# Three banks in turn for the third layer of the first expert, the conversions among them

## The chip, the core and the metric

The kernel runs on one core of a Trainium2 chip. Four of the core's engines compute: TensorE (PE in the profile; its weight loads are PEld), VectorE (DVE), ScalarE (ACT) and GpSimd (POOL). SyncE (SP) and POOL also issue transfers. PE writes its products to PSUM, a small memory of eight banks, from which DVE and ACT read. The metric is the device time of one launch in microseconds.

## What is computed

Three stages, each fed by the one before. Stage two sends each of 3072 tokens to one of eight experts of 384 tokens each, and every expert passes two matrices; stage three passes the tokens through two more, with a rational function between. The kernel does stages two and three expert by expert.

```python
# 1: attention with a decaying state, y of shape (4, 8, 768, 64)
state = gamma * state + outer(k[t], v[t]);  y[t] = scale * q[t] @ state
# 2: experts, x of shape (3072, 512); a greedy choice by x @ w_gate, 384 tokens each
h = np.maximum(x[mask] @ w1[e], 0.0)        # 512 -> 1024
out[mask] = h @ w2[e]                       # 1024 -> 512
# 3: rational network
h = x @ w_in                                # 512 -> 2048
P = a[0] + a[1] * h + a[2] * h2 + a[3] * h3
Q = 1.0 + np.abs(b[0]) * np.abs(h) + np.abs(b[1]) * h2
g = P / (Q + 1e-06)
out = g @ w_out                             # 2048 -> 512
```

## The kernel before

**Stages.** The first 168 us are the attention; the routing follows, and then eight experts, n = 0 to 7. Each matrix product is made of three passes over numbers split in a high and a low part (`split`, `three`). An expert has two halves. In the first, `mm1` (w1) and `mm2` (w2) alternate over 8 blocks of 128 columns. In the second, `mm3` (w_in) and `mm4` (w_out) run over 16 blocks i: `mm3(n, i)` writes one PSUM bank of 128x384; `rat1` to `rat3` and `gsplit` make the rational function of it; `mm4(n, i - 3)` uses the result three blocks later. PE's round is therefore mm3 of block i, mm4 of block i - 3.

**A block's way.** mm3 is 12 matmuls at L840. ACT reads the bank three times (L894 to L896). POOL adds (L897). DVE reads the bank twice (L898, L899); the bank is free when L899 has ended. Meanwhile ACT makes a reciprocal by logarithm and exponential (L908, L909), DVE refines and applies it (L914 to L916), ACT and POOL split the result (L921, L922), and mm4 (L936) takes it.

**Banks.** Of the eight banks four are sums (`acc0` to `acc3`), one is for the routing (`pr`), two have the name `w` and one the name `x`. `wtile` hands out `w` and `x`: it counts in `WN[0]`, and each third tile is `x`, so that three banks take turns. With `first=True`, which `mm1` and `mm3` of the first expert pass, it doesn't count and always gives one of the two `w`.

**Conversions.** Weights arrive as 64-bit numbers. Most blocks of w_in are converted in the attention stage; the six blocks in `NORES` (5, 7, ... 15) are converted in the first expert's second half, between its blocks: `in_conv_a(j)` calls `conv`, which works on DVE in three steps (L243, L245 and L246, in the profile CUSTOM_DVE_ANT_0) with one step on ACT (L244). Its middle value is in the bank that `ctile` gives, which is `x`; L243 and L245 write it, L246 reads it last. `in_conv_b` splits the result (L249 on ACT, L250 on POOL) into the tile `wis`, which the block's mm3 reads, and `in_store` sends it to memory for the later experts. Conversion j is asked for behind block 1 + 2j.

**The next expert.** While an expert runs, the routing for the next is chosen in small steps (`Chain`): PE's L641, L654, L690 and L691, L721, L731 and, on DVE, the rows between L576 and L745; its products lie in `pr`. `xt` transposes the next expert's tokens (L824 to L827) behind blocks 12 to 14; for expert 1 it asks for `x`.

**Order.** PE, ACT and POOL run in the order of the program as written. The order on DVE and SP is made by a scheduler, which knows what each instruction waits for; the routing's steps have a raised priority. A bank that is handed out again is waited for by its next writer until its last reader has ended.

Of the kernel before, what the change touches and what calls it, by code (L numbers as in the profile page):

```python
# [9 lines left out]
F32 = mybir.dt.float32  # L10
# [19 lines left out]
CAP = NT // E  # L30
# [5 lines left out]
KD = DM // 128  # L36
# [140 lines left out]
def moe_kernel(ctx, tc, q, k, v, w_gate, w1, w2, w_in, w_out, a, b, cf, ci, out):  # L177
# [363 lines left out]
    ps = ctx.enter_context(tc.tile_pool(name="ps", bufs=1, space=bass.MemoryType.PSUM))  # L541
# [229 lines left out]
    EV, W1R, W2R, W1S, W2S, XG, XTS, HS, YS, ACC, US, GS, WIS = ({} for _ in range(13))  # L771
# [34 lines left out]
    WN = [0]  # L806

    def wtile(shape, first=False):


        if not first:
            WN[0] += 1
        x = not first and WN[0] % 3 == 0
        return ps.tile(shape, F32, name="x" if x else "w", bufs=1 if x else 2)
# [4 lines left out]
    def xt(n, t):  # L819
        if t == 0:  # L820
            XTS[n] = mp.tile([128, 2, KD, CAP], F32R, name="xT", bufs=1)
        p = ps.tile([128, KD, 128], F32, name="x", bufs=1) if n == 1 else wtile([128, KD, 128])
        for d in range(KD):
            nc.tensor.transpose(p[:, d, :], XG[n][t][:, d * 128:(d + 1) * 128], ident)  # L824
        hi = XTS[n][:, 0, :, t * 128:(t + 1) * 128]
        nc.scalar.activation(hi, p, AF.Copy)  # L826
        nc.vector.tensor_tensor(XTS[n][:, 1, :, t * 128:(t + 1) * 128], p, hi.bitcast(F32), op=OP.subtract)  # L827

    def three(prods, first, last, split=True):

        jobs = [(k, a, b) for k in range(len(prods)) for a, b in ((0, 0), (1, 0), (0, 1))]
        if split:
            jobs.sort(key=lambda t: t[2])
        n = {}
        for k, a, b in jobs:
            o, w, x = prods[k]
            key = id(o)
            n[key] = n.get(key, 0) + 1
            total = 3 * sum(1 for p in prods if p[0] is o)
            nc.tensor.matmul(o, w[a], x[b], start=first and n[key] == 1, stop=last and n[key] == total)  # L840
# [3 lines left out]
    def mm1(n, f):  # L844
        p = wtile([128, CAP], n == 0)
        w, x = W1S[n, f], XTS[n]
        three([(p, (w[:, 0, d * 128:d * 128 + 128], w[:, 1, d * 128:d * 128 + 128]), (x[:, 0, d], x[:, 1, d]))
               for d in range(KD)], True, True)
        h = HS[n, f] = mp.tile([128, 2, CAP], F32R, name="hg", bufs=HGB)
        nc.scalar.activation(h[:, 0], p, AF.Relu)  # L850
        HLO[n, f] = nc.vector.scalar_tensor_tensor(h[:, 1], p, 0.0, h[:, 0].bitcast(F32), op0=OP.max,  # L851
                                                   op1=OP.subtract).ins
        w1_split(n, f + 2)

    def mm2(n, f):
        if f == 0:
            for t in (3, 0, 1, 2):
                ACC[t] = ps.tile([128, 512], F32, name=f"acc{t}")
        w, h = W2S[n, f], HS[n, f]
        three([(ACC[(d + 3) % 4][:, :CAP], (w[:, 0, d * 128:d * 128 + 128], w[:, 1, d * 128:d * 128 + 128]),  # L860
                (h[:, 0], h[:, 1])) for d in range(KD)], f == 0, f == NF1 - 1, f < NF1 - 1)
        w2_split(n, f + 2)
        if f == NF1 - 1:
            y = YS[n] = mp.tile([128, 2, KD, CAP], F32R, name="yT", bufs=1)
            for d in range(KD):
                p = ACC[(d + 3) % 4][:, :CAP]
                nc.scalar.activation(y[:, 0, d], p, AF.Copy)
                nc.vector.tensor_tensor(y[:, 1, d], p, y[:, 0, d].bitcast(F32), op=OP.subtract)

    def wi_load(n, j):  # L870
        if j >= len(NORES):
            return
        i = NORES[j]
        t = WIS[n, i] = mp.tile([128, 2, KD, 128], F32R, name="wis", bufs=NWIS)
        nc.gpsimd.dma_start(t.rearrange("p s a f -> p (s a f)"), wid[i])

    def mm3(n, i):
        p = US[n, i] = wtile([128, CAP], n == 0)
        y = YS[n]
        w = wih[:, RES[i]] if i in RES else WIS[n, i]  # L880
        three([(p, (w[:, 0, d], w[:, 1, d]), (y[:, 0, d], y[:, 1, d])) for d in range(KD)], True, True)
        if n and i not in RES:
            wi_load(n, NORES.index(i) + NWIS)
# [88 lines left out]
    def job_conv(j):  # L972
        if j < NLATE:
            CA[j] = mp.tile([128, KD * 128], I32, name="xg", bufs=TB)
            conv(rawx[:, j % 3], CA[j], mp.tile([128, KD * 128], I32, name="xg", bufs=TB), ctile())
            job_load(j + 3)

    def job_split(j):
        if 0 <= j < NLATE:
            split(woh[:, LATE_OUT[j]], CA[j].bitcast(F32), nc.gpsimd)  # L980
# [3 lines left out]
    def in_load(j):  # L984
        if j >= len(NORES):
            return
        i = NORES[j]
        t = RX[j] = mp.tile([128, KD * 128, 2], I32, name="w2s")
        nc.sync.dma_start(t.bitcast(I64).rearrange("p (a f) o -> p a (f o)", a=KD),
                          w_in[:, i * 128:(i + 1) * 128].rearrange("(a p) f -> p a f", p=128))  # L990

    def in_conv_a(j):
        if j >= len(NORES):
            return
        CA[j] = mp.tile([128, KD * 128], I32, name="w2r")
        conv(RX[j], CA[j], mp.tile([128, KD * 128], I32, name="w2r"), ctile())
        in_load(j + 2)

    def in_conv_b(j):
        i = NORES[j]  # L1000
        w = WIS[0, i] = mp.tile([128, 2, KD, 128], F32R, name="wis", bufs=NWIS)
        w = w.rearrange("p s a f -> p s (a f)")
        split(w, CA[j].bitcast(F32), nc.gpsimd)

    def in_store(j):
        i = NORES[j]
        nc.gpsimd.dma_start(wid[i], WIS[0, i].rearrange("p s a f -> p (s a f)"))
# [27 lines left out]
    def slot(part):  # L1035
        nonlocal credit
        credit += RATE[min(len(ROUTE), 2) - 1][part]
        if credit >= 1:
            credit -= 1
            chain.hop()  # L1040

    for n in range(E):
        last = n + 1 == E
        for f in range(NF1):
            mm2(n, f)
            slot(0)
            if n == 0:
                job_split(f - 1)
                with tc.issue_after(HLO[0, min(f + 1, NF1 - 1)]):
                    job_conv(f)  # L1050
            if f + 2 < NF1:
                mm1(n, f + 2)
                slot(0)
        if n == 0:
            for j in range(2):
                in_load(j)
            for i in range(INA):
                if i in NORES:
                    in_conv_a(NORES.index(i))
            for i in range(INB):  # L1060
                if i in NORES:
                    in_conv_b(NORES.index(i))
            for i in range(INS):
                if i in NORES:
                    in_store(NORES.index(i))
        else:
            for j in range(NWIS):
                wi_load(n, j)
        for i in range(NF2):
            if i > 1:  # L1070
                gsplit(n, i - 2)
            if i:
                rat2(n, i - 1)
                rat3(n, i - 1)
            mm3(n, i)
            slot(1)
            rat1(n, i)
            if i >= LAG:
                mm4(n, i - LAG)
                slot(1)  # L1080
            if n == 0 and i + INA in NORES:
                in_conv_a(NORES.index(i + INA))
            if n == 0 and i + INB in NORES:
                in_conv_b(NORES.index(i + INB))
            if n == 0 and i + INS in NORES:
                in_store(NORES.index(i + INS))
            if n == 0 and i == NF2 - 2:
                for f in range(2):
                    w2_load(1, f)
            if not last:  # L1090
                if i == DUE:
                    begin(n + 1)
                if i - DUE in (0, 1, 2):
                    fetch(n + 1, i - DUE)
                if i - DUE in (2, 3):
                    w1_split(n + 1, i - DUE - 2)
                if i - DUE in (2, 3, 4):
                    xt(n + 1, i - DUE - 2)
        gsplit(n, NF2 - 2)
        rat2(n, NF2 - 1)  # L1100
        rat3(n, NF2 - 1)
        gsplit(n, NF2 - 1)
        for i in range(NF2 - LAG, NF2):
            f = i - NF2 + LAG
            if not last and f < 2:
                mm1(n + 1, f)
                w2_split(n + 1, f)
                slot(1)
            mm4(n, i)
            slot(1)  # L1110
# [26 lines left out]
```

## Time and profile before

| | us |
|---|---|
| time, median of 3 runs | 1068.32 (1067.13 to 1068.67) |
| the profiled execution's own time | 1068.97 |
| its span, from first to last instruction | 1066.0 |
| PE busy | 1008.1 (95%) |
| DVE busy | 758.7 (71%) |
| ACT busy | 697.3 (65%) |
| POOL busy | 622.7 (58%) |

Busy is the time in which an engine works on an instruction; PE counts as busy also where its clock is low. Busy shares are means over stages, so a stage is read from its own stretch of the timeline. The mean granted clock of PE is 0.979 of full speed. The first expert's second half runs from 238.8 to about 318 us.

### The profile page before, as it was taken

To read this page: it belongs to the slowest core of one execution; us is meant where nothing else is said; L and a number is where in the kernel's file an instruction comes from. 1 tells how busy PE (TensorE), PEld (TensorE's weight loads), DVE (VectorE), ACT (ScalarE), POOL (GpSimd) and SP (SyncE) were. 2 spreads that over 40 slices of the span, in tenths; PEclk is the share of its full clock that TensorE was granted. 3 is DMA by queue.
4 is the path that set the end of the run, shared out by engine and by line. 5 is a ranking of instruction groups with operands and counts; after the bars stand their busy time and mean duration, and the time that the engine had idled before them with its cause. 6 is when DMAs were issued, how large, how long until landed. Compare 5 with 4: busy or idle time off the path is not lost.

```text
span 1066.0 us, 18253 instructions
## 1 busy us (share of the span) xinstructions
PE 1008.1 (95%) x6278; PEld 922.1 (87%) x6278; DVE 758.7 (71%) x1841; ACT 697.3 (65%) x1365; POOL 622.7 (58%) x612
## 2 busy tenths in 40 slices
PE   6999994798999999999999999999999999999995
PEld 5888884687789988999899989998999899889984
DVE  4788797579975887588657875887678656751773
ACT  6989991357773687367736873687367737873883
POOL 5667661555685466546654665466546654675452
PEclk9999996799999999999999999999999999999998
DMA  9999963433333221322132223222412241323110
GB/s 193 226 261 259 247 154 108 150 99 102 106 118 110 80 89 58 112 80 89 60 110 79 89 61 113 75 90 59 139 50 91 60 136 53 97 68 118 34 60 30
DMA packets 142027, 115.00 MB, mean 108 GB/s; under 512 B 56560, under 2 KB 122352, under 8 KB 141936
## 3 DMA queue, kind: packets, MB, share of 16 engines
q1 hardware_dynamic: 131184, 76.10, 27.3%
q0 software_dynamic: 10752, 37.75, 10.8%
q8 instruction: 49, 0.80, 0.3%
q14 instruction: 42, 0.34, 0.1%
HBM read 98.10 MB, written 15.73 MB: 107 GB/s over the span
## 4 chain that ended last, share of the span: by engine, by line
PE 72%; DVE 10%; ACT 4%; issue 2%; DMA 1%; POOL 1%; POOLq 0%; DVEq 0%; ACTq 0%
PE w L840 24%; PE acc L936 24%; PE x L840 10%; PE acc L840 8%; PE pr L641 1%; DVE cm L605 1%; DVE hg L851 1%; ACT hg L850 1%; PE pa L384 1%; PE pt L354 1%; PE pr L619 0%; PE w L824 0%; PE x L824 0%; DVE t L898 0%; DVE t L916 0%
## 5 line engine op out<-in xcount | busy, mean ns | idle before, releaser
L936 PE MATMUL acc<-woh,hg 128*128 128x512 f32 x1152 | 289.3, 396 | 0.8 <-ACT hg L921 0.8
L936 PEld LDWEIGHTS acc<-woh,hg 128*128 128x128 f32 x1152 | 213.4, 188 | 43.5 <-ACT hg L921 1.8
L897 POOL TENSOR_TENSOR qq<-qq,z 128x384 f32<-128x384 f32 x127 | 129.0, 1016 | 166.8 <-ACT z L895 165.8
L922 POOL TENSOR_TENSOR hg<-t,hg 128x384 fp32r<-128x384 f32 x127 | 129.5, 1020 | 77.4 <-ACT hg L921 49.0
L840 PE MATMUL acc<-hg,w2s 128*128 128x384 f32 x768 | 145.9, 339 | 0.3 <-DVE hg L851 0.3
L840 PEld LDWEIGHTS acc<-hg,w2s 128*128 128x128 f32 x768 | 132.4, 188 | 1.1 <-DVE hg L851 0.6
L840 PE MATMUL w<-yT,wih 128*128 128x384 f32 x624 | 117.9, 339 | 0.9 <-DVE t L899 0.8
L840 PE MATMUL w<-xT,w1s 128*128 128x384 f32 x600 | 116.6, 343 | 0.6 <-ACT xT L826 0.6
L914 DVE SCALAR_TENSOR_TENSOR qq<-qq,acc 128x384 f32<-128x384 f32 x128 | 70.8, 553 | 59.3 <-ACT acc L909 29.9
L840 PEld LDWEIGHTS w<-yT,wih 128*128 128x128 f32 x624 | 108.1, 188 | 3.6 <-DVE t L899 1.8
L250 POOL TENSOR_TENSOR w1s<-w1r,w1s 128x512 fp32r<-128x512 f32 x64 | 82.6, 1291 | 46.8 <-ACT w1s L249 46.0
L250 POOL TENSOR_TENSOR w2s<-w2r,w2s 128x512 fp32r<-128x512 f32 x64 | 82.6, 1292 | 44.6 <-ACT w2s L249 41.3
L840 PEld LDWEIGHTS w<-xT,w1s 128*128 128x128 f32 x600 | 105.9, 192 | 1.9 <-ACT xT L826 0.8
L921 ACT ACTIVATE hg<-t 128x384 fp32r<-128x384 f32 x128 | 67.2, 525 | 57.7 <-DVE t L916 57.6
L249 ACT ACTIVATE w2s<-w2r 128x512 fp32r<-128x512 f32 x64 | 40.2, 629 | 67.2 <-issue 37.7
L908 ACT ACTIVATE z<-qq,qcb 128x384 f32<-128x384 f32 x128 | 77.7, 607 | 7.9 <-POOL qq L897 7.3
L840 PE MATMUL w<-yT,wis 128*128 128x384 f32 x408 | 78.1, 339 | 3.2 <-DVE t L899 3.2
L916 DVE SCALAR_TENSOR_TENSOR t<-t,ab,acc 128x384 f32<-128x384 f32 x128 | 78.4, 613 | 3.4
L840 PEld LDWEIGHTS w<-yT,wis 128*128 128x128 f32 x408 | 70.9, 188 | 5.8 <-DVE t L899 4.2
L915 DVE SCALAR_TENSOR_TENSOR acc<-qq,acc 128x384 f32<-128x384 f32 x128 | 71.6, 560 | 3.3
L850 ACT ACTIVATE hg<-w 128x384 fp32r<-128x384 f32 x50 | 24.5, 489 | 65.7 <-PE w L840 64.1
L909 ACT ACTIVATE acc<-z 128x384 f32<-128x384 f32 x128 | 63.5, 496 | 4.1
(200 smaller groups left out, 1967.2 us busy)
## 6 DMA issues: line engine op xcount, KB each, us to landing
wis<-wid POOLq DMA_DIRECT2D x42, 512.0 KB, 3.6
w1r<-in_moe_w_dram SPq DMA_DIRECT2D x64, 256.0 KB, 2.8
w2r<-in_moe_w_dram SPq DMA_DIRECT2D x64, 256.0 KB, 2.7
qn<-in_q_dram SPq DMA_DIRECT2D x48, 128.0 KB, 4.4
kn<-in_k_dram SPq DMA_DIRECT2D x24, 256.0 KB, 4.6
vn<-in_v_dram SPq DMA_DIRECT2D x24, 256.0 KB, 5.2
xd<-xn SPq DMA_DIRECT2D x48, 128.0 KB, 4.2
raw<-in_moe_w_in_dram SPq DMA_DIRECT2D x10, 512.0 KB, 5.9
```

The source lines that it names most:

```text
L249: nc.scalar.activation(dst[:, 0], src, AF.Copy)
L250: lo_eng.tensor_tensor(dst[:, 1], src, dst[:, 0].bitcast(F32), op=OP.subtract)
L840: nc.tensor.matmul(o, w[a], x[b], start=first and n[key] == 1, stop=last and n[key] == total)
L897: light(n, i).tensor_tensor(qq, qq, z, op=OP.add)
L908: nc.scalar.activation(z, qq, AF.Ln, bias=qcb)
L909: nc.scalar.activation(r[:, :CAP], z, AF.Exp, scale=-1.0)
L914: nc.vector.scalar_tensor_tensor(qq, qq, QC, r, op0=OP.add, op1=OP.mult)
L915: nc.vector.scalar_tensor_tensor(r, qq, 2.0, r, op0=OP.subtract, op1=OP.mult, reverse0=True)
L916: nc.vector.scalar_tensor_tensor(t, t, ab[:, 0:1], r, op0=OP.add, op1=OP.mult)
L921: nc.scalar.activation(g[:, 0], t, AF.Copy)
L922: light(n, i).tensor_tensor(g[:, 1], t, g[:, 0].bitcast(F32), op=OP.subtract)
L936: nc.tensor.matmul(ACC[t], g[:, x, t * 128:(t + 1) * 128], woh[:, i, y], start=i == 0 and x + y == 0, stop=i == NF2 - 1 and x == 1)
```

## The change

Three edits: `mm3` no longer passes `n == 0`, so the first expert's third layer counts in `wtile` as the later experts' do; `WN[0]` is set to 2 ahead of that half, so that block 0 gets `x`, blocks 1 and 2 get `w`, block 3 gets `x`, and so on; and `xt` takes `wtile`'s turn for expert 1 too. The conversions still ask for `x`.

```diff
--- before.py
+++ after.py
@@ -819,7 +819,7 @@
     def xt(n, t):
         if t == 0:
             XTS[n] = mp.tile([128, 2, KD, CAP], F32R, name="xT", bufs=1)
-        p = ps.tile([128, KD, 128], F32, name="x", bufs=1) if n == 1 else wtile([128, KD, 128])
+        p = wtile([128, KD, 128])
         for d in range(KD):
             nc.tensor.transpose(p[:, d, :], XG[n][t][:, d * 128:(d + 1) * 128], ident)
         hi = XTS[n][:, 0, :, t * 128:(t + 1) * 128]
@@ -875,7 +875,7 @@
         nc.gpsimd.dma_start(t.rearrange("p s a f -> p (s a f)"), wid[i])
 
     def mm3(n, i):
-        p = US[n, i] = wtile([128, CAP], n == 0)
+        p = US[n, i] = wtile([128, CAP])
         y = YS[n]
         w = wih[:, RES[i]] if i in RES else WIS[n, i]
         three([(p, (w[:, 0, d], w[:, 1, d]), (y[:, 0, d], y[:, 1, d])) for d in range(KD)], True, True)
@@ -1052,6 +1052,8 @@
                 mm1(n, f + 2)
                 slot(0)
         if n == 0:
+
+            WN[0] = 2
             for j in range(2):
                 in_load(j)
             for i in range(INA):
```

Where instructions stand. DVE at blocks 0 and 1, before: from L914 of block 0 to the end of the first conversion. `t_3283` and `qq_3282` belong to block 0, `t_3311` to block 1, `x_3320` is the first conversion's bank (its L243 and L245 stand ten and eight rows above the first row here, on either side of L649), `acc3` holds the reciprocal.

```order
L914 SCALAR_TENSOR_TENSOR qq_3282<-qq_3282,acc3_3290 128x384
L915 SCALAR_TENSOR_TENSOR acc3_3290<-qq_3282,acc3_3290 128x384
L898 TENSOR_TENSOR t_3311<-w_3296,t_3311 128x384
L916 SCALAR_TENSOR_TENSOR t_3283<-t_3283,ab_66,acc3_3290 128x384
L899 SCALAR_TENSOR_TENSOR t_3311<-t_3311,ab_66,w_3296 128x384
L246 ISA w2r_3318<-x_3320,w2r_3319 128x1024
```

The same place now, with the two conversion steps inside it and a routing step (L648 to L650) as well:

```order
L914 SCALAR_TENSOR_TENSOR qq_3282<-qq_3282,acc3_3290 128x384
L243 TENSOR_SCALAR x_3320<-w2s_3257 128x512
L915 SCALAR_TENSOR_TENSOR acc3_3290<-qq_3282,acc3_3290 128x384
L898 TENSOR_TENSOR t_3311<-w_3296,t_3311 128x384
L916 SCALAR_TENSOR_TENSOR t_3283<-t_3283,ab_66,acc3_3290 128x384
L648 TENSOR_TENSOR cmk_3352<-pr_2481,cft_64 64x128
L899 SCALAR_TENSOR_TENSOR t_3311<-t_3311,ab_66,w_3296 128x384
L649 TENSOR_REDUCE ce_3353<-cmk_3352 64x16
L245 SCALAR_TENSOR_TENSOR x_3320<-w2s_3257,x_3320 128x512
L650 TENSOR_TENSOR ex_2486<-ce_3353,pr_2481 64x128
L246 ISA w2r_3318<-x_3320,w2r_3319 128x1024
```

The conversion's first two steps moved from ahead of block 0's L898 to behind its L899, since they write the bank that block 0 now has.

DVE at the third conversion, before: the rows up to its last step, L246 (`w2r_3540<-x_3542`). `t_3465` belongs to block 4, `t_3508` to block 5; L703 to L712 are the routing's. The conversion's L243 and L245 stand nine and four rows above the first row here, both ahead of L701.

```order
L914 SCALAR_TENSOR_TENSOR qq_3464<-qq_3464,acc3_3487 128x384
L703 TENSOR_TENSOR u_3527<-sl_3526 128x24
L745 SCALAR_TENSOR_TENSOR Sl_68<-eo_3697,Sl_68 128x192
L706 TENSOR_SCALAR ua_3528<-u_3527 128x24
L707 TENSOR_SCALAR ua_3528<-u_3527 128x24
L915 SCALAR_TENSOR_TENSOR acc3_3487<-qq_3464,acc3_3487 128x384
L709 TENSOR_TENSOR L_3529<-ua_3528,cit_65 128x384
L714 TENSOR_TENSOR BH_3531<-ua_3528,cit_65 128x576
L712 TENSOR_TENSOR LV_3530<-L_3529,cit_65 128x384
L916 SCALAR_TENSOR_TENSOR t_3465<-t_3465,ab_66,acc3_3487 128x384
L898 TENSOR_TENSOR t_3508<-w_3493,t_3508 128x384
L246 ISA w2r_3540<-x_3542,w2r_3541 128x1024
```

The same place now; ahead of its first row stand L701, L243 and L702, in that order:

```order
L245 SCALAR_TENSOR_TENSOR x_3542<-w2s_3325,x_3542 128x512
L703 TENSOR_TENSOR u_3527<-sl_3526 128x24
L914 SCALAR_TENSOR_TENSOR qq_3464<-qq_3464,acc3_3487 128x384
L706 TENSOR_SCALAR ua_3528<-u_3527 128x24
L707 TENSOR_SCALAR ua_3528<-u_3527 128x24
L915 SCALAR_TENSOR_TENSOR acc3_3487<-qq_3464,acc3_3487 128x384
L709 TENSOR_TENSOR L_3529<-ua_3528,cit_65 128x384
L714 TENSOR_TENSOR BH_3531<-ua_3528,cit_65 128x576
L712 TENSOR_TENSOR LV_3530<-L_3529,cit_65 128x384
L916 SCALAR_TENSOR_TENSOR t_3465<-t_3465,ab_66,acc3_3487 128x384
L898 TENSOR_TENSOR t_3508<-w_3493,t_3508 128x384
L246 ISA w2r_3540<-x_3542,w2r_3541 128x1024
```

L243 and L245 of the third conversion moved behind L701, which waits for PE's L691; L246 kept its place behind block 5's L898.

PE at block 6, the difference (before and now):

```order
@@ -590,5 +590,5 @@
 L690 MATMUL pr<-X,umor 128x48
 L691 MATMUL pr<-X,oner 128x48
-L840 MATMUL w<-yT,wih 128x384 x12
+L840 MATMUL x<-yT,wih 128x384 x12
 L936 MATMUL acc_3400<-woh,hg 128x512
 L936 MATMUL acc_3401<-woh,hg 128x512
```

PE's order stayed; block 6 now writes `x`, whose user ahead of it in the program is the third conversion.

## Rows read from the trace of the kernel before

**Rows 1.** The page: busy time and share of the span by engine.
```profile
PE 1008.1 (95%) x6278; PEld 922.1 (87%) x6278; DVE 758.7 (71%) x1841; ACT 697.3 (65%) x1365; POOL 622.7 (58%) x612
```

**Rows 2.** PE's waits: total us, times, longest.
```profile
PE w L840 <- DVE t L899: 4.0, 5, 1.5
```

**Rows 3.** PE's timeline: start, us, what, count, [idle before <-releaser].
```profile
238.84 2.30 PE L840 MATMUL w<-yT,wih 128*128 128x384 f32 x12
242.18 0.33 PE L654 MATMUL pr<-ex,oner 128*128 128x128 f32 x1 [1.04 <-DVE ex L650]
...
245.02 2.36 PE L840 MATMUL w<-yT,wih 128*128 128x384 f32 x12 [0.38 <-DVE t L899]
...
247.98 2.38 PE L840 MATMUL w<-yT,wih 128*128 128x384 f32 x12 [0.43 <-DVE t L899]
...
252.35 2.30 PE L840 MATMUL w<-yT,wih 128*128 128x384 f32 x12
254.50 2.27 PE L936 MATMUL acc<-woh,hg 128*128 128x512 f32 x9
257.30 2.35 PE L840 MATMUL w<-yT,wis 128*128 128x384 f32 x12 [0.54 <-DVE t L899]
...
261.62 0.27 PE L691 MATMUL pr<-X,oner 128*128 128x48 f32 x1
...
286.86 2.35 PE L840 MATMUL w<-yT,wis 128*128 128x384 f32 x12 [1.19 <-DVE t L899]
```

**Rows 4.** ACT's timeline, block 0.
```profile
241.18 0.58 ACT L894 ACTIVATE qq<-w,rb 128x384 f32<-128x384 f32 x1 [1.82 <-PE w L840]
...
242.12 0.67 ACT L896 ACTIVATE t<-w,ab 128x384 f32<-128x384 f32 x1
...
244.00 0.50 ACT L909 ACTIVATE acc<-z 128x384 f32<-128x384 f32 x1
```

**Rows 5.** DVE's timeline, 248 to 294 us.
```profile
248.44 0.27 DVE L648 TENSOR_TENSOR cmk<-pr,cft 64x128 f32<-64x128 f32 x1
...
249.24 0.36 DVE L649 TENSOR_REDUCE ce<-cmk 64x16 f32<-64x128 f32 x1
...
249.98 0.27 DVE L650 TENSOR_TENSOR ex<-ce,pr 64x128 fp32r<-64x128 f32 x1
...
258.35 0.54 DVE L914 SCALAR_TENSOR_TENSOR qq<-qq,acc 128x384 f32<-128x384 f32 x1
258.81 0.68 DVE L243 TENSOR_SCALAR x<-w2s 128x512 int32<-128x512 int32 x1
...
259.87 0.55 DVE L898 TENSOR_TENSOR t<-w,t 128x384 f32<-128x384 f32 x1
...
261.38 0.68 DVE L245 SCALAR_TENSOR_TENSOR x<-w2s,x 128x512 int32<-128x512 int32 x1
261.98 0.24 DVE L701 TENSOR_TENSOR_SCAN sl<-pr,zero 128x48 f32<-128x48 f32 x1
262.15 0.47 DVE L742 TENSOR_SCALAR eo<-c,em 128x8 f32<-128x8 f32 x1
...
263.21 0.35 DVE L745 SCALAR_TENSOR_TENSOR Sl<-eo,Sl 128x192 f32<-128x192 f32 x1
...
266.37 0.68 DVE L246 CUSTOM_DVE_ANT_0 w2r<-x,w2r 128x1024 uint16<-128x1024 uint16 x1
...
293.98 0.68 DVE L246 CUSTOM_DVE_ANT_0 w2r<-x,w2r 128x1024 uint16<-128x1024 uint16 x1
```

**Rows 6.** DVE in one stretch: length, busy us, granted clock, DMA.
```profile
240.00:310.00 70.00, 66.03 (x157) 1.00 0.37 117
```

**Rows 7.** PE's timeline in the attention stage.
```profile
61.15 0.66 PE L413 MATMUL py<-am,vt 128*64 128x128 f32 x8 [1.77 <-DVE am L386]
62.34 1.01 PE L413 MATMUL py<-am,vt 128*64 128x128 f32 x8 [0.54 <-DVE am L386]
```

**Rows 8.** PE in one stretch: length, busy us, granted clock, DMA.
```profile
62.00:66.00 4.00, 3.65 (x21) 0.57 1.09 285
```

## Prediction

> **What bounds the kernel now.** The page comes first: TensorE (PE) is busy for 95% of the span, VectorE (DVE) for 71% [rows 1]. That is a mean over stages. The change touches one stage only, the first expert's second half, so the views after the page are cut to it: PE's waits, then PE's timeline of 238 to 312 us, then those of DVE and ScalarE (ACT) beside it. In PE's waits, blocks of the third layer wait five times for L899, DVE's last reader of a block's bank, 4.0 us in total [rows 2]. PE's timeline has the first of the five at 245.02 and the last at 286.86, and they stand at blocks 2, 3, 5, 7 and 11 [rows 3]; the later experts, which take turns with three banks, have none. One more wait stands there: 1.04 us at L654, for a small step of the routing that DVE finishes late [rows 3]. In these 70 us DVE is busy for 66.03 [rows 6]. So here DVE, and the order in which it works, says when banks come free, and PE runs on what it leaves.
>
> **What the change removes.** Block b is mm3(0, b); c0 to c5 are the six conversions, asked for behind blocks 1, 3, 5, 7, 9 and 11. With three banks a block no longer needs the reader of the block two before it: the five waits, 4.0 us, go. In the new DVE order the two conversion steps that stood among L648, L649 and L650 are gone from there, so L654's operand is ready while block 0 still runs, and its 1.04 us go too. Removed: 5.0 us. No instruction is added or dropped on any engine; PE, ACT and POOL (GpSimd) keep their order, and SP moves one load of a conversion behind a load of the next expert, with several blocks to spare before its use (cost nothing; the fourth conversion stands between).
>
> **What it adds.** The third bank x used to serve the conversions and the next expert's transposes. Its users are now, in the order of the program: b0, c0, b3, c1, c2, b6, c3, b9, c4, c5, b12, a transpose, b15. So b3 must wait until c0's last step (L246, on DVE) has read x, b6 until c2's, b9 until c3's, b12 until c5's. Before, nothing on PE waited for a conversion's hold of x here. A DVE row's place costs its duration less 0.08 us, as rows of 0.54 and 0.68 show whose next row starts 0.46 and 0.60 after them (258.35, 261.38) [rows 5].
>
> Block 3. PE runs b0, b1 and b2 without a wait from 238.84, each 2.15 to the next (252.35 to 254.50 [rows 3]), with 0.06 for L654 and 0.17 for L641: it wants b3 at 245.5. DVE: b0's reciprocal is out when L909 ends, at 244.50 [rows 4]; then follow, by the new order, L914, L243, L915, L898, L916, L899 and L245, which took 258.35 to 261.98, 3.63 us, where they stand next to each other in the trace, then L648, L649, L650 (0.19 + 0.28 + 0.19), and L246, 0.68 [rows 5]. That is 4.97 us, so x is free at 249.5, and with 0.05 us for the signal **b3 waits 4.0 us**.
>
> Block 6. From b3's start to L691's end took 247.98 to 261.89, and 0.54 of it was b5's wait [rows 3]: 13.37 us. Added to 249.57 that is 262.94; PE starts 0.16 before a row's end and wants b6 at 262.8. In the new DVE order L701, which needs L691, stands ahead of c2's steps, and c2's last step stands 14 rows behind L701. So whenever PE gets there, it must wait for this stretch. In the trace the stretch from L701 to L246's end took 261.98 to 267.05, 5.07 us; L742 and L745 leave it (0.39 + 0.27), L243 and L245 come in (0.60 each) [rows 5]: 5.61. DVE can be there: from the row behind c0's last step, at 248.44, to L701 took 13.5 us [rows 5], of which L648 to L650 and c2's L243 and L245, 1.9 us, are now elsewhere, so 11.7 against the 13.4 that PE takes. x is free at 268.6: **b6 waits 5.9 us**.
>
> Block 12. c5 is asked for behind b11, and its last step stands right behind b11's L899. From b11's start: its matmuls 2.30, three ACT rows 1.61 [rows 4], on DVE L898, L916 and L899, 259.87 to 261.38, 1.51, and L246, 0.68 [rows 5], and three signals of 0.04: 6.2 us. PE has b11 and one block of the fourth layer to do in that time, 2.15 + 2.10 [rows 3]: **b12 waits 2.0 us**. Where ACT lags, as it did before, it is more: there the same L246 ended at 294.66, 7.8 us behind b11's start at 286.86 [rows 3, 5], which would make 3.5. I take 2.0, since ACT catches up during the two long waits; 1 to 3.5 stays in the range.
>
> Hidden: b9 needs c3, whose last step stands two rows behind b7's L899, about 6.3 us behind b7's start; PE has two rounds, 8.5 us, until b9. If that cover went, it would cost up to 2 us. b15 needs a transpose's reader from a round and a half before.
>
> Sum without the clock: 4.0 + 5.9 + 2.0 − 5.0 = +6.9 us. PE's order is the same after this stage and its blocks there follow each other without such waits, so the shift stays to the end.
>
> **The clock.** Long waits cost PE a second time. At 61.15 and 62.34 us PE had waited 1.77 and 0.54, and between 62 and 66 us the granted clock was 0.57 on the mean, the level of 1.2 GHz for most of it, so 4 × 0.43 = 1.7 us of full speed were lost [rows 7, 8]. Waits of 4.0 and 5.9 are longer than those. Bounds: nothing, if PE's work on both sides keeps the clock at 2.4 GHz or the slow stretch lies wholly within the waits, and 3.4 for two full stretches as above; a third would make 5.1. I take 2.2, since a slow stretch lies in part inside a wait, where it costs nothing. The Trainium skill (TensorE: Matmul & The Clock Gate, "What's actually happening") says that the slow clock is the default and that activity releases it; that goes with this row, and by it the term is nearer its upper than its lower bound.
>
> The sum: 6.9 + 2.2 = +9.1. The profiled execution took 1068.97 with a span of 1066.0, so 3.0 lie around it: 1075.1 span, 1078.1. That execution is 0.65 above the median of the runs, 1068.32; against the median: 1077.4, said as 1077.
>
> **The rivals.** *Banks come free in time (faster).* If c0's and c2's last steps came before PE wants x, only the removed waits would count: 1068.3 − 5.0 = 1063.3. It decides at c0: its L246 would have to end at 245.5, though it cannot start its first step before L899 of b0 and, by the order, L914 at 244.5. For it speaks that the later experts rotate through the same three banks without a wait; against, that no conversion takes turns with them there. The Trainium skill (Perfetto Trace Analysis, "Matmuls") asks for just such a rotation of independent groups through banks, so that emptying one overlaps the next; by that alone this case would be the likely one.
>
> *DVE alone sets the stage (no change).* DVE works 66.03 of 70 us here [rows 6] and the change gives it no more to do. If it went on without a gap, the waits would only be moved: 1068.3, and less than 4 us either way. Against it: while PE waits for c2, ACT and DVE soon have no block to work on, so DVE's idle time grows by what PE waits. It decides at whether DVE has work behind L246 of c2; by the order it has b5's L899 and b5's last three rows, about 2 us, and a block needs 2.30 + 1.61 before DVE sees it.
>
> *Half clock for longer.* Three or more slow stretches, and the lag at b12: 6.9 + 1.5 + 5.1 = +13.5, 1081.8.
>
> That the change does not do what it says is out: the order shows b0, b3, ... b15 in x.
>
> **How the numbers follow.** Forecast 0.82, faster 0.06, no change 0.06, half clock for longer 0.06. A measurement of this kernel can tell about 0.2%, 2.1 us, from no change. Faster by more than that 0.06; within it 0.06; slower by more 0.88. The likeliest is 1077. The low end is the forecast with each of the three waits 1 us shorter and no clock lost, 1068.3 + 3.9 = 1072.2, less a little for the no-change case: 1071.5. The high end is the lag at b12 and a slow stretch more: 1068.3 + 6.9 + 1.5 + 4.3 = 1081.
>
> **What would show it.** In the new trace PE's waits should name L246 as what b3, b6 and b12 waited for, 3 to 5, 5 to 7 and 1 to 3.5 us, and no longer L899 or L650 in this stage. The first block of the next expert should start 6 to 11 us later than before, with the granted clock under 1.00 somewhere in 246 to 275. From there to the end both traces should be as long as each other. The forecast is wrong if b3 starts before 247, if DVE's rows between L701 and L246 do not stand as ordered, or if the time comes back behind 320 us.

## The result and the profile after

| | before | now |
|---|---|---|
| time, median of 4 runs each | 1067.89 us (1067.13 to 1068.67) | 1079.41 us (1077.12 to 1080.40) |
| the profiled execution's own time | 1068.97 | 1077.12 |
| its span | 1066.0 | 1075.2 |
| start of block 0 | 238.84 | 237.22 |
| first block of the next expert | 309.51 | 318.27 |
| between the two, called the stage below | 70.67 | 81.05 |

The ratio is 1.0103, with a 95% interval of 1.0091 to 1.0115: the change makes the kernel 11.5 us slower.

The page's busy times answer to [rows 1]; with none of PE's work changed, they hardly move, and would not show where the time went:

```profile
PE 1010.3 (94%) x6278; PEld 924.7 (86%) x6278; DVE 762.5 (71%) x1841; ACT 697.4 (65%) x1365; POOL 622.8 (58%) x612
```

PE's waits do (total us, times, longest). The row that stands where [rows 2] stood; no wait for L899 or L650 is left in this stage:

```profile
PE x L840 <- DVE w2r L246: 11.8, 3, 6.0
```

PE's timeline, as in [rows 3] (start, us, what, count, [idle before <-releaser]):

```profile
237.22 2.30 PE L840 MATMUL x<-yT,wih 128*128 128x384 f32 x12
...
239.45 4.38 PE L840 MATMUL w<-yT,wih 128*128 128x384 f32 x24
...
248.04 3.75 PE L840 MATMUL x<-yT,wih 128*128 128x384 f32 x12 [4.03 <-DVE w2r L246]
...
253.96 2.30 PE L840 MATMUL w<-yT,wih 128*128 128x384 f32 x12
...
258.20 2.25 PE L840 MATMUL w<-yT,wis 128*128 128x384 f32 x12
...
262.42 0.27 PE L691 MATMUL pr<-X,oner 128*128 128x48 f32 x1
268.66 4.10 PE L840 MATMUL x<-yT,wih 128*128 128x384 f32 x12 [5.97 <-DVE w2r L246]
...
274.69 2.25 PE L840 MATMUL w<-yT,wis 128*128 128x384 f32 x12
...
292.06 2.30 PE L840 MATMUL w<-yT,wis 128*128 128x384 f32 x12
...
298.31 2.97 PE L840 MATMUL x<-yT,wih 128*128 128x384 f32 x12 [1.85 <-DVE w2r L246]
...
304.57 2.33 PE L840 MATMUL w<-yT,wis 128*128 128x384 f32 x12
...
318.27 2.24 PE L840 MATMUL w<-xT,w1s 128*128 128x384 f32 x12
```

Blocks 0, 1 and 2 run without a gap (237.22 and the 24 matmuls from 239.45). Then b3, b6 and b12 wait for a conversion's last step. In the same rows, the twelve matmuls of a block take 3.75, 4.10 and 2.97 us behind each wait, against 2.30 for block 0: the clock. PE in stretches of 4 us that lie behind the three waits (length, busy, granted clock, DMA share, GB/s):

```profile
248.00:252.00 4.00, 3.96 (x13) 0.57 0.47 131
...
268.00:272.00 4.00, 3.34 (x10) 0.50 0.73 246
...
300.00:304.00 4.00, 4.00 (x14) 0.60 0.13 48
```

0.50 is the 1.2 GHz level, 1.00 the 2.4 GHz level; the other two stretches lie partly at each. On DVE, where block 6's wait is decided:

```profile
262.72 0.26 DVE L701 TENSOR_TENSOR_SCAN sl<-pr,zero 128x48 f32<-128x48 f32 x1 [0.20 <-PE pr L691]
262.90 0.67 DVE L243 TENSOR_SCALAR x<-w2s 128x512 int32<-128x512 int32 x1
...
263.61 0.69 DVE L245 SCALAR_TENSOR_TENSOR x<-w2s,x 128x512 int32<-128x512 int32 x1
...
267.46 0.54 DVE L898 TENSOR_TENSOR t<-w,t 128x384 f32<-128x384 f32 x1
267.93 0.68 DVE L246 CUSTOM_DVE_ANT_0 w2r<-x,w2r 128x1024 uint16<-128x1024 uint16 x1
```

From L701 to L246's end DVE works almost without a gap, 5.89 us, on rows of the routing, of block 4 and of block 5, while PE stands. While PE stands, no new block comes, so DVE runs dry behind this: its busy time over the 70 us of [rows 6] falls from 66.03 to:

```profile
240.00:310.00 70.00, 59.07 (x134) 0.90 0.30 93
```

### The profile page after: what moved, and what is told of

Same layout as the page of the kernel before. It is cut to its first block, busy times and chain, and to the rows that moved or that the text cites. A ratio compares the mean times of both kernels' runs of the same rounds, so it can differ in the third digit from the quotient of the medians.

```text
span 1075.2 us, 18254 instructions
## 1 busy us (share of the span) xinstructions
PE 1010.3 (94%) x6278; PEld 924.7 (86%) x6278; DVE 762.5 (71%) x1841; ACT 697.4 (65%) x1365; POOL 622.8 (58%) x612
## 4 chain that ended last, share of the span: by engine, by line
PE 71%; DVE 9%; ACT 2%; issue 2%; POOL 1%; DMA 0%; POOLq 0%; DVEq 0%; ACTq 0%
PE acc L936 24%; PE w L840 23%; PE x L840 11%; PE acc L840 8%; PE pr L641 1%; DVE cm L605 1%; DVE hg L851 1%; ACT hg L850 1%; PE w L824 1%; PE pr L619 0%; DVE x L245 0%; PE x L824 0%; DVE t L898 0%; POOL qq L897 0%; DVE x L243 0%
## 5 line engine op out<-in xcount | busy, mean ns | idle before, releaser
L914 DVE SCALAR_TENSOR_TENSOR qq<-qq,acc 128x384 f32<-128x384 f32 x128 | 70.9, 554 | 61.8 <-ACT acc L909 29.3
L840 PE MATMUL w<-yT,wih 128*128 128x384 f32 x576 | 108.2, 339 | 0.0
L921 ACT ACTIVATE hg<-t 128x384 fp32r<-128x384 f32 x128 | 67.2, 525 | 58.3 <-DVE t L916 58.2
L840 PEld LDWEIGHTS w<-yT,wih 128*128 128x128 f32 x576 | 100.0, 188 | 1.7
L840 PE MATMUL x<-yT,wih 128*128 128x384 f32 x384 | 77.3, 352 | 12.0 <-DVE w2r L246 11.8
L840 PEld LDWEIGHTS x<-yT,wih 128*128 128x128 f32 x384 | 69.9, 197 | 14.5 <-DVE w2r L246 12.5
L916 DVE SCALAR_TENSOR_TENSOR t<-t,ab,acc 128x384 f32<-128x384 f32 x128 | 78.5, 613 | 3.5
L840 PE MATMUL w<-yT,wis 128*128 128x384 f32 x384 | 73.1, 338 | 0.0
L840 PEld LDWEIGHTS w<-yT,wis 128*128 128x128 f32 x384 | 66.9, 188 | 1.8
```

Source lines behind the costliest of these rows:

```text
L914: nc.vector.scalar_tensor_tensor(qq, qq, QC, r, op0=OP.add, op1=OP.mult)
L916: nc.vector.scalar_tensor_tensor(t, t, ab[:, 0:1], r, op0=OP.add, op1=OP.mult)
L921: nc.scalar.activation(g[:, 0], t, AF.Copy)
```

## Where the 10.4 us of the stage come from

The distances between starts of blocks, now less before. Two are clean: to b6 +6.03 (wait 5.97) and to b12 +1.97 (wait 1.85); before, these two blocks started at 261.73 and 291.14, behind b5 at 257.30 and b11 at 286.86 [rows 3]:

```profile
261.73 2.33 PE L840 MATMUL w<-yT,wih 128*128 128x384 f32 x12
...
291.14 2.25 PE L840 MATMUL w<-yT,wih 128*128 128x384 f32 x12
```

With b3's row, 4.03, the **added waits** are 12.0 us. The **clock** is read from the round behind each wait, against the same round in an experiment below in which it ran at full clock: 5.92 against 4.35 at b3, 6.03 against 4.30 at b6, 6.26 against 4.71 at b12, together 4.9 us. The stage grew by 10.38, so 12.0 + 4.9 − 10.4 = 6.5 us were **removed**, as the remainder; the rows of the waits that went add up to 5.0, but each distance shrank by more than its wait's row (1.27 for 1.04, 0.57 for 0.38, 0.71 for 0.54, 1.45 for 1.19).

Behind the stage both traces are equally long to 0.4 us (1075.2 − 318.27 = 756.9; 1066.0 − 309.51 = 756.5). Ahead of it the new one is 1.6 us shorter, since its attention has no slow stretch like that of [rows 8] (e1, e6 and e8 below have one there, at 60 to 68 us, e4 and e13 have none). So the profiled span grew by 9.2 only. The other three runs of the changed kernel have spans 1.8 to 3.3 us longer than the profiled one, at granted clocks of 0.972, 0.972 and 0.973 against its 0.974; 0.0015 of 1075 us is 1.6 us of full speed, so slow stretches elsewhere may be a part of it. No trace of these runs shows where they lie.

## The experiments

The theory: a conversion holds the bank x until its last step, L246, and this step stands late in DVE's order; the turn that comes to x waits for it, and its wait costs PE the clock. The rivals: the banks have nothing to do with it, since DVE is full and sets the stage; or one of the three edits alone does the harm. All ratios are to runs of the kernel before on the same chip.

| kernel | time (us) | ratio, 95% interval | stage (us) |
|---|---|---|---|
| now | 1079.41 | 1.0103 (1.0091 to 1.0115) | 81.05 |
| e1: now, conversions without a bank | 1071.96 | 1.0036 (1.0022 to 1.0050) | 76.38 |
| e4: before, conversions without a bank | 1069.34 | 1.0015 (1.0006 to 1.0025) | 71.85 |
| e2: before, with the edit of xt | 1073.27 | 1.0045 (1.0028 to 1.0062) | 76.81 |
| e3: now, turns shifted by one | 1078.90 | 1.0105 (1.0088 to 1.0122) | 81.74 |
| e7: now, three of six conversions in x | 1077.88 | 1.0098 (1.0081 to 1.0114) | 82.03 |
| e6: now, conversions first on DVE | 1072.69 | 1.0047 (1.0030 to 1.0064) | 75.71 |
| e8: now, conversions earlier and first | 1071.02 | 1.0026 (1.0014 to 1.0037) | 73.15 |
| e5: now, PE filled at b6 and b12 | 1078.23 | 1.0091 (1.0071 to 1.0111) | 79.84 |
| e5b: now, PE filled at b12 | 1078.30 | 1.0104 (1.0087 to 1.0120) | 80.63 |
| e13: e1, a block's rows first on DVE | 1072.37 | 1.0045 (1.0028 to 1.0061) | 74.95 |

The stage is that of the profiled execution, whose own time can lie some 2 us from the median of its kernel (e1 1074.14, e2 1075.28, e13 1070.62).

**The conversions out of the banks: e1 in the kernel now, e4 in the kernel before.** The middle value goes to SBUF.

```diff
-        conv(RX[j], CA[j], mp.tile([128, KD * 128], I32, name="w2r"), ctile())
+        conv(RX[j], CA[j], mp.tile([128, KD * 128], I32, name="w2r"))
```

> The changed kernel, but the six conversions keep their middle value in the SBUF tile that they write at the end, not in bank x. Theory 1 (blocks wait because conversions hold the bank whose turn it is): no wait for L246 any more, no slow stretch of the clock between 240 and 310 us, the time falls by 10 to 14 us to 1065 to 1069. It does not fall far below the kernel before, since DVE's work here stays the bound. Theory 2 (the new order on DVE is what costs, whoever has the bank): 1076 to 1080, with waits of 4 and 6 us at blocks 3 and 6 for other DVE rows. Theory 3 (three banks gain the 5 us that the kernel before waited, once nothing shares them): 1061 to 1063.

> The kernel before (two banks in turn) with the conversions' middle value in SBUF, as the earlier run had it with three banks (1072.0). The pair shows what three banks are worth where nothing shares them. If DVE is the bound of this stage, its rows are what counts and the two are alike: 1069 to 1073 here. If a third bank of its own gains what the kernel before waits for banks, this one is 4 to 6 us slower than with three: 1076 to 1078.

In e1 every wait for L246 is gone, and 7.5 of the 11.5 us with them. The time lies between what theory 1 (1065 to 1069) and theory 2 (1076 to 1080) gave: the stage is still 5.7 us longer than before, with a slow stretch of the clock at its end (0.71 on the mean from 304 to 308 us). PE's waits in e1, 236 to 322 us:

```profile
PE acc L936 <- ACT hg L921: 3.7, 5, 1.5
PE x L824 <- DVE t L899: 2.2, 1, 2.2
PE w L840 <- DVE t L899: 1.0, 1, 1.0
```

Other waits came, all for steps that hang on DVE's rows, and DVE is as busy as before (65.85 of 70 us). So the sharing is the larger part of the harm, and the third bank brings nothing even without it: three banks (e1) are 2.6 us slower than two (e4) by the medians, 2.2 by the ratios, whose intervals just touch. The third bank's loss against e4 lies at b12 to b15, where the transposes now take turns in the same banks (7.13, 7.05 and 6.38 us between starts, against 4.62, 4.62 and 4.82 in e4); the next run shows this edit by itself. A part of it isn't the banks': ahead of b12's rows on DVE a small step of the routing, L596, took 3.02 us in e1 and 0.84 in e4, and the wait of 2.2 us is for b12's L899 behind it. The last section comes back to L596. In e13 below, with three banks too, it took 0.17, and other DVE rows were stretched in its place. e4 itself is 1.6 us slower than the kernel before and has nothing to gain: the conversions' bank was in nobody's way before, and its three DVE steps take as long in sum (the last section).

**The edit of xt alone: e2.**

```diff
-        p = ps.tile([128, KD, 128], F32, name="x", bufs=1) if n == 1 else wtile([128, KD, 128])
+        p = wtile([128, KD, 128])
```

> The kernel before with the smallest of the three edits alone: the transposes for expert 1 take wtile's turn, so two of three use a w bank, while mm3 keeps its two w banks. Theory 1 (a bank's next user waits for its last reader): blocks 13 to 15 and the transposes now share two w banks, block 14 waits 1 to 3 us for L899 of the block right ahead, 1069 to 1071. Rival (this edit does nothing by itself): 1067 to 1068.5.

It was worse than expected, 5.2 us against the kernel before on its chip, and the wait came at block 13, not at 14. PE's timeline, DVE's, and PE in a stretch of 4 us:

```profile
300.60 4.21 PE L840 MATMUL w<-yT,wis 128*128 128x384 f32 x12 [3.14 <-DVE t L899]
```

```profile
299.02 1.01 DVE L596 SCALAR_TENSOR_TENSOR pr<-ni,cit 128x16 int32<-128x16 int32 x1
299.95 0.60 DVE L899 SCALAR_TENSOR_TENSOR t<-t,ab,w 128x384 f32<-128x384 f32 x1
```

```profile
302.00:306.00 4.00, 4.00 (x13) 0.50 0.41 124
```

The first transpose takes one of the two w between b12 and b13, so b13 needs the bank of b12 and waits until DVE's last reader of it ends at 300.55; half clock follows. With the transposes in x, as before, b13 gets the bank of b11. In the kernel now this wait does not show, since b12 is in x there.

**Other turns: e3.** Blocks 1, 4, 7, 10 and 13 take x in place of 0, 3, 6, 9, 12 and 15.

```diff
-            WN[0] = 2
+            WN[0] = 1
```

(and one more count behind the half, so that the later experts' turns stay).

> The changed kernel with the turn moved by one: blocks 1, 4, 7, 10 and 13 have bank x, and the count is set right again behind the loop. The conversions asked for right ahead of such a block are now the second (ahead of block 4) and the fifth (ahead of block 10). Theory 1: waits for L246 at blocks 4 and 10 and none at 3, 6 and 12; about 8 us at block 4, because the second conversion is asked for behind block 3 and stands far down in DVE's order, 2 to 3 us at block 10; the sum as long as before or up to 2 us more than the changed kernel's 11.9; 1076 to 1081. Theory 2 (DVE's order or the routing's rows at those places, not the turn): waits stay near blocks 3, 6 and 12.

PE's waits and the longer one in PE's timeline:

```profile
PE x L840 <- DVE w2r L246: 12.6, 2, 8.9
```

```profile
257.80 4.21 PE L840 MATMUL x<-yT,wih 128*128 128x384 f32 x12 [8.87 <-DVE w2r L246]
```

The waits left b3, b6 and b12 and stand at b4 (8.87) and b10 (3.69), the turns that now come to x while a conversion holds it. They move with the turns, which a DVE that is simply full does not explain.

**Fewer conversions in x: e7.** c0, c2 and c5, the three that were waited for, go to SBUF.

```diff
-        conv(RX[j], CA[j], mp.tile([128, KD * 128], I32, name="w2r"), ctile())
+        conv(RX[j], CA[j], mp.tile([128, KD * 128], I32, name="w2r"), ctile() if j in (1, 3, 4) else None)
```

> The changed kernel, where only the three conversions that blocks 3, 6 and 12 waited for (first, third, sixth) keep their middle value in SBUF; the other three still use bank x. Theory 1, by the turn alone: block 6 now waits for the second conversion, long done, block 12 for the fifth, and block 9 for the fourth, so no long wait is left: 1070 to 1073 like the run with all six in SBUF. Theory 1 with DVE's order: this kernel's order has the fourth conversion's steps right behind block 7's L899, and block 9 may wait up to 6 us where DVE is late: 1073 to 1077. Theory 2 (not the bank): 1078 or more.

The three waits went and two others came, at b6 1.42 and here at b9, in PE's and DVE's timelines:

```profile
281.45 4.21 PE L840 MATMUL x<-yT,wis 128*128 128x384 f32 x12 [6.22 <-DVE w2r L246]
```

```profile
278.60 0.68 DVE L243 TENSOR_SCALAR x<-w2s 128x512 int32<-128x512 int32 x1
...
279.65 0.68 DVE L245 SCALAR_TENSOR_TENSOR x<-w2s,x 128x512 int32<-128x512 int32 x1
...
280.72 0.68 DVE L246 CUSTOM_DVE_ANT_0 w2r<-x,w2r 128x1024 uint16<-128x1024 uint16 x1
```

c3, which was in time before, now stands 6 us too late: the scheduler laid DVE's order out anew, and L243 comes only at 278.60, behind block 7's L899 and many rows of the routing. The time, 1077.88, is above the 1073 to 1077 of theory 1 and next to the 1078 of theory 2, so the time by itself doesn't decide; the rows do. What theory 1 had not reckoned with stands at the end of the stage: b14 to b15 takes 8.45 us in place of 4.82, with two more waits for DVE (1.13 and 1.88) behind an L596 of 5.58 us. It is not these three conversions; it is where L246 stands in DVE's order when a turn comes to its bank.

**The place in DVE's order alone: e6 and e8.** In e6 the conversions' DVE steps have a raised priority; in e8 they are also asked for behind blocks 0, 3, 4, 7, 9 and 10. Banks and turns are those of the kernel now.

```diff
-                in_conv_a(NORES.index(i + INA))
+                with tc.high_priority(offset=PRIO):
+                    in_conv_a(NORES.index(i + INA))
```

> The changed kernel with the first steps of the conversions (in_conv_a) at the routing's raised priority, so that DVE takes their rows earlier; banks and turns are the same. Theory 1 (the wait is the place of L246 in DVE's order): the first conversion's L246 stands 4 rows behind block 0's L914 instead of 10, so block 3 waits about 2 us, not 4; the third conversion's steps still stand around the routing's L701, so block 6 keeps 5 to 6 and block 12 1.5 to 2; 1075 to 1078. Theory 2 (the number of rows on DVE is what counts): same waits in sum, 1078.5 to 1080.5.

> The kernel after with the same three banks in turn and the conversions in the shared bank, but the conversions asked for behind blocks 0, 3, 4, 7, 9 and 10 in place of 1, 3, 5, 7, 9 and 11, ahead of the other small steps of a block, and with a raised priority in DVE's order. If the added time comes from how late in DVE's order the last step of a conversion stands, the three long waits (4.03, 5.97 and 1.85 us) fall to 1 to 2 us each, a fourth of about 1 us may come at block 9, at most one slow stretch of the clock stays, and the time is 1068 to 1072. If the conversions in the rotation cost their time wherever they stand, because DVE is full, DVE's other rows come later by as much, PE waits for L899 or L916 in place of L246, and the time stays at 1073 to 1079.

e6's waits are 2.05, 6.44 and 1.20, in sum 2.2 us less than in the kernel now, yet it is 6.7 us faster, 5.3 of them in the stage: two of the three slow stretches went too (b3 to b4 takes 4.35, b12 to b13 4.70), which makes 3.1. That is more than was expected of it (1075 to 1078). PE's waits in e8, its rows for them, and two stretches of 4 us:

```profile
PE x L840 <- DVE w2r L246: 6.0, 4, 2.6
PE w L840 <- DVE xT L827: 0.4, 1, 0.4
```

```profile
247.64 2.35 PE L840 MATMUL x<-yT,wih 128*128 128x384 f32 x12 [1.31 <-DVE w2r L246]
...
263.28 3.01 PE L840 MATMUL x<-yT,wih 128*128 128x384 f32 x12 [2.56 <-DVE w2r L246]
...
293.18 2.35 PE L840 MATMUL x<-yT,wih 128*128 128x384 f32 x12 [1.99 <-DVE w2r L246]
```

```profile
264.00:268.00 4.00, 4.00 (x15) 0.59 0.73 247
...
292.00:296.00 4.00, 2.82 (x15) 1.00 0.22 66
```

With nothing changed but when the conversions' steps run, three quarters of the loss are gone. This settles the theory against the rival that DVE alone sets the time: DVE is busy for 69.4 us of the stage in the kernel now and for 68.7 in e8, and the stage is 7.9 us shorter. What is left in e8 against the kernel before, 2.5 us of the stage, is in the main 6.4 us of waits against 5.0, and the one slow round (b6 to b7 5.84 against 4.30).

**The clock by itself: e5 and e5b.** PE gets products with zero rows, added to a sum, ahead of b6 (24, in e5 alone) and of b12 (6 in both), so that it works where it waited.

```diff
+            if n == 0:
+                fill(i)
             mm3(n, i)
```

> The changed kernel with useless work for PE in two of its three waits: 24 products of zeros (128 x 512) ahead of block 6 and 6 ahead of block 12, added to a sum that they leave as it is, about 5.1 and 1.3 us long. Banks come free as before. Theory 1a (part of the loss is PE's low clock behind a wait): PE's clock stays at 1.00 behind blocks 6 and 12, the blocks there take 2.15 instead of 3.9 and 2.8 us, and the time falls by 2.5 to 3.5 us, to 1076 to 1077, with more work done. Theory 1b (DVE sets the pace behind a wait anyway, PE's clock costs nothing): 1079 to 1080 as the changed kernel, or more by the added work.

> The changed kernel with 6 products of zeros on PE ahead of block 12 alone (about 1.3 of its 1.85 us of waiting). DVE's order is that of the changed kernel row by row, which it was not in the run with both fillings. Theory 1a (PE's low clock behind a wait is a loss of its own): the clock stays at 1.00 behind block 12, block 12 to block 13 takes 4.7 in place of 6.3 us, and this stays to the end: 1077.3 to 1078.3. Theory 1b (DVE sets the pace there): 1079 to 1080.

PE's rows for b6 of e5, and for b12 of e5b:

```profile
270.45 2.35 PE L840 MATMUL x<-yT,wih 128*128 128x384 f32 x12 [0.30 <-DVE w2r L246]
```

```profile
299.80 2.35 PE L840 MATMUL x<-yT,wih 128*128 128x384 f32 x12 [0.27 <-DVE w2r L246]
```

Twelve matmuls take 2.35 us, not 4.10 or 2.97, and the rounds behind take 4.30 and 4.71: the slow rounds came from PE standing idle. But the time gains little: e5 is 1.2 us faster than the kernel now by the medians, less than the 2.5 to 3.5 expected, and e5b's ratio is that of the kernel now. In e5b, whose DVE order is that of the kernel now, b14 to b15 takes 5.92 against 4.82, with a transpose that waits 0.7 us for L899. So of 1.55 us given back by the clock about 1.1 are lost again two rounds later to DVE, where L596 took 4.58 us ahead of that L899, against 2.99 in the kernel now. PE at full clock runs into the next bound here.

**An attempt at a better version: e13.** e1, with DVE's five rows of a block (L898, L899, L914 to L916) at a raised priority in the first expert.

> The kernel after with the conversions' middle value in SBUF, so that the three banks are the blocks' alone, and DVE's five rows of a block (L898, L899, L914 to L916) of the first expert at a raised priority. If the third bank is worth something once no conversion holds it and DVE takes a block's rows first, the second half of the first expert is shorter than before, 67 to 70 us against 70.67, and the time is 1065 to 1068. If DVE's work alone sets this half, about 66 of 70 us, the order of its rows gains nothing: 70 to 76 us and 1068 to 1073, with PE waiting for ACT's hg or for L899 at the last blocks.

It is no faster than e1: the medians differ by 0.4 us, as the second half of the expectation has it. PE's longest wait and the row of it; then DVE ahead of it:

```profile
PE acc L936 <- ACT hg L921: 5.7, 3, 4.6
```

```profile
284.40 4.21 PE L936 MATMUL acc<-woh,hg 128*128 128x512 f32 x9 [4.55 <-ACT hg L921]
```

```profile
277.55 1.42 DVE L245 SCALAR_TENSOR_TENSOR w2r<-w2s,w2r 128x512 int32<-128x512 int32 x1
...
280.69 1.65 DVE L245 SCALAR_TENSOR_TENSOR w2r<-w2s,w2r 128x512 int32<-128x512 int32 x1
...
283.20 0.60 DVE L916 SCALAR_TENSOR_TENSOR t<-t,ab,acc 128x384 f32<-128x384 f32 x1
```

Two conversions stand back to back ahead of a block's L916, which ACT's L921 needs, with L245 at twice its length. None of the versions beats the kernel before.

## Why the prediction held, point by point

- **What bounds the stage** held: DVE's order says when banks come free.
- **Block 3**: 4.0 predicted, 4.03 measured. x was free 10.76 us behind block 0's start; the working gave 10.66.
- **Block 6**: 5.9 and 5.97. From L701 to L246's end 5.61 was worked out, 5.89 measured.
- **Block 12**: 2.0 and 1.85. From b11's start to L246's end 6.2 was worked out, 6.19 measured (292.06 to 298.25). The choice that ACT catches up during the long waits was right, so the 3.5 did not come.
- **b9 and b15** were hidden, as said.
- **Removed**: 5.0 predicted, 6.5 measured (the remainder above). The term took the waits' own rows. A PE row that needn't wait also starts ahead of the end of the row in front of it, by the 0.16 that the working used elsewhere; at six places that makes 1.0 of the 1.5. The rest is spread over small gaps.
- **The clock** is the term that was mis-sized: 2.2 taken, 4.9 measured, at the upper bound for three stretches (5.1). The step that failed is "a slow stretch lies in part inside a wait, where it costs nothing". That was so at b6 only in part (the clock in 264 to 268 us has a mean of 0.71 there, PE idle), and at b3 and b12 not at all; and a third stretch followed the shortest wait, 1.85 us, which the sum had left to a rival of 0.06. The 4.9 is by how much the rounds got longer, not what the kernel would win: given back at b12 it was worth 0.4 us of the stage (e5b), at b6 and b12 1.2 (e5).
- **The sum**: 9.1 predicted, 10.4 measured in the stage, 11.5 between the medians (of four runs each; the forecast started from 1068.32, the median of three); 1079.41 lies within the range, 2.4 above the forecast. The errors of the removed waits and of the clock, −1.5 and +2.7, partly cancel. About 1 us between stage and medians is not settled.
- **Rivals.** *Banks come free in time* fell at the point named: c0's L246 could not end before b3 wanted x. But its 1063.3 was wrong even for its own case: e1 has no such waits and the blocks still don't run through, because DVE's other rows and the transposes come next. *DVE alone sets the stage* fell as the cause of the loss (e8), and is the likely reason why the third bank won nothing in these versions: over the stage itself DVE is busy for 94% before (66.7 of 70.67 us) and in e8, 93% in e1 and e13, and 86% in the kernel now. That is argued and not shown, for a part of this busy time is rows that are stretched beside POOL (the last section). *Half clock for longer* had its third stretch, and not its lag at b12.

## What to carry to other kernels

Before a rotation gets another buffer, list every user of it in the order of the program, and find the last reader of each user on the engine that runs in order: what counts is where that row stands in the other engine's order when the turn comes, not how short it is. A long job in a rotation of short ones wants its steps first in that order, or a buffer outside the rotation; and a user kept on a buffer of its own, as the transposes were, may be what keeps two neighbours apart. Where the engine behind the buffers is busy for 94% of the stage (66.03 of 70 us), more buffers only moved the wait, and the price of a long wait on PE has to hold the slow round behind it.

## What was not expected of the hardware

**Short waits and the clock.** In this stage a round that was in part at half clock, 1.4 to 2.6 us longer, followed waits of 1.85 (the kernel now, b12), 1.88 (e7, ahead of b15), 2.17 (e1, ahead of b14), 2.56 (e8, b6), 3.14 (e2, b13) and of all longer ones; none followed 1.31 and 1.99 (e8, b3 and b12), 2.05 (e6, b3) or 1.42 (e7, b6). So the wait's length alone doesn't sort them, and these traces don't show what does.

**DVE beside POOL.** With its middle value in SBUF the same step of a conversion takes at times twice as long. The group of L245 in the kernel now, and in e1 (busy us, mean ns):

```profile
L245 DVE SCALAR_TENSOR_TENSOR x<-w2s,x 128x512 int32<-128x512 int32 x6 | 4.1, 686 | 0.0
```

```profile
L245 DVE SCALAR_TENSOR_TENSOR w2r<-w2s,w2r 128x512 int32<-128x512 int32 x6 | 5.4, 898 | 0.0
```

One of the six of e1 on DVE, and what POOL does then:

```profile
253.12 1.47 DVE L245 SCALAR_TENSOR_TENSOR w2r<-w2s,w2r 128x512 int32<-128x512 int32 x1
```

```profile
253.01 1.02 POOL L922 TENSOR_TENSOR hg<-t,hg 128x384 fp32r<-128x384 f32 x1
```

POOL's row began 0.11 us ahead and ended at 254.03; DVE's then needed 0.56 more, near its usual 0.68. The Trainium skill (SBUF — State Buffer, "SBUF: two separate sides") says that a DVE instruction with two SBUF inputs and a GpSimd instruction that reads SBUF shut each other out for the whole of the earlier one. The trace agrees: with one operand in PSUM the six take 0.686 on the mean, with both in SBUF 0.898. So a bank that only holds a middle value also keeps DVE out of POOL's way. In e4 the first step, L243, gets shorter by the move (538 ns on the mean against 684), L245 and L246 longer (797 and 742 against 687 and 683): 12.5 us in sum against 12.3.

One row of DVE was stretched far more, and it bears on the experiments. L596, a step of the routing on 128x16 numbers with both operands in SBUF, has a median of 0.18 us over its seven runs in each trace. In this stage it took 1.03 us before, 2.99 in the kernel now, 3.02 in e1, 4.58 in e5b and 5.58 in e7, but 0.18 in e6 and 0.17 in e13. DVE in the kernel now, POOL in the kernel now, and DVE in e5b:

```profile
306.27 2.99 DVE L596 SCALAR_TENSOR_TENSOR pr<-ni,cit 128x16 int32<-128x16 int32 x1
```

```profile
308.19 1.01 POOL L897 TENSOR_TENSOR qq<-qq,z 128x384 f32<-128x384 f32 x1
```

```profile
306.21 4.58 DVE L596 SCALAR_TENSOR_TENSOR pr<-ni,cit 128x16 int32<-128x16 int32 x1
```

In the kernel now it starts beside the first of three POOL rows that follow each other without a gap, and ends at 309.26, 0.06 us behind the third. Wherever it is long, its end lies within 0.2 us behind the end of a POOL row; in e6 and e13 it starts just behind one. So a short row of DVE can be held up beside more than one row of POOL. That is read from these times; no run takes POOL's rows away there.
